# Where the key and query products of the first three pairs land in PSUM, and an early one-column Exp, in a fused attention and feed-forward kernel

## The chip, the cores and the metric

The kernel runs on one core of one Trainium2 chip. The metric is the device time of one execution in microseconds. A profiled execution gives, besides its time, a trace: every instruction of the engines TensorE (PE, with its weight loads as PEld), VectorE (DVE), ScalarE (ACT), GpSimd (POOL) and SyncE (SP) with its start, its length and what it waited for.

## What is computed

The input x has 2048 rows of 448 values in bf16. After a layer norm, two branches run side by side and are added to x. Branch A is linear attention with 16 heads of 28 and a learned feature map; branch B is a feed-forward block with SiLU.

```python
xn = _layernorm(x)
return x + _A_ref(xn, A_wqkv, A_w_phi, A_wo) + _B_ref(xn, B_w1, B_w2)
# A: q, k, v = heads of xn @ wqkv
pq = einsum("bhsd,hdf->bhsf", q, w_phi);  pk = einsum("bhsd,hdf->bhsf", k, w_phi)
phi_q = concat([softmax(pq), softmax(-pq)]);  phi_k = concat([softmax(pk), softmax(-pk)])
kv = einsum("bhsf,bhsd->bhfd", phi_k, v);  z = einsum("bhsf->bhf", phi_k)
o = einsum(phi_q, kv) / (einsum(phi_q, z) + 1e-6);  return o @ wo
# B
return silu(xn @ w1) @ w2
```

## The kernel before

**Tiles and stages.** The 2048 rows are 8 pairs of two tiles of 128 rows. Stage one loads x and w1, normalises the pairs, transposes them (xnT) and computes the first feed-forward product for pairs 0 to 5, with a SiLU on ScalarE after every unit (function ffn1_chunk). In between, w_phi is folded into the weights of queries and keys (fold), so that one product gives pk and one pq. Stage two, the one that the change touches, goes once through the pairs 0 to 7. Stage three multiplies queries with the key-value sums, divides, transposes, and adds the second feed-forward product and the product with wo, pair by pair, and stores.

**One pair of stage two.** k_macro (L877) makes three things. The keys of the pair: 14 matmuls of 448 columns in two passes of row halves (proj, contract), into two PSUM banks; then two Exps on ScalarE (exp_act, L776), one of the values and one of their negatives, out of these banks into a slot of scr or wraw (Ek). The values: 14 matmuls into banks 2 and 3, copied out by VectorE (L469). The sums of the exponentials on VectorE (L892), their reciprocals (L894), and the scaling on POOL (L900). q_group (L922) makes the queries of a group of heads c for half of all rows (pairs 0 to 3, then 4 to 7): 14 matmuls of 512 columns into two banks and two Exps into EqT. From pair 3 on, every second pair also accumulates keys with values for two earlier pairs in bank 4 (k_acc). All matmuls are issued by the helper mms (L446), all operations of ScalarE by act (L465).

**The banks.** Of the eight PSUM banks, values always have 2 and 3. Keys have 0 and 1, only those of pair 1 have 4 and 5. Queries always have 6 and 7. Bank 4 is free until the accumulation of keys with values begins in pair 3. A matmul that writes a bank anew waits until all readers of that bank's old content are through: for keys and queries that is the second of their two Exps.

**What sets the order.** The program collects operations with their data dependences; a planner orders them per engine from estimated costs. TensorE's order is tied down by a chain written out by hand: in a pair, the first pass of the keys, the first of the values, the second of the keys, the second of the values (in even pairs and in pair 1 its last step stands behind the queries' first pass), then the queries' two passes; in pairs 3, 5 and 7 the accumulation stands between the queries' two passes. On ScalarE, Exps carry order ties behind all earlier SiLUs, and later SiLUs behind the Exps, so that the function tables are switched once each way. The build puts a table load ahead of the first operation that needs another table; where that operation waits for a semaphore, the wait stands ahead of the load. The loads of w2 and wo on SyncE's queue wait for the first Exp of the keys of pairs 0 to 4.

**Names.** neghalf is a small constant tile that POOL fills at the start, and pre a two-column scratch tile: a one-column Sqrt from neghalf to pre's first column runs at the start of ScalarE's queue. silus and exps collect the SiLUs and Exps so far.

Of the kernel before, what the change touches and what calls it, by code (L numbers as in the profile page):

```python
# [8 lines left out]
ACTF = mybir.ActivationFunctionType  # L9
# [99 lines left out]
def _cols(ap):  # L109
    n = 1  # L110
    for st, cnt in list(ap.ap)[1:]:
        n *= cnt
    return n
# [219 lines left out]
def bass_parallel_sum__linear_kernel_hedgehog__dense_activation_silu__prompt_kernel(  # L333
# [21 lines left out]
    with es:  # L355
        def sb(name, shape, dt):
            return es.enter_context(nc.sbuf_tensor(name, shape, dt))
# [29 lines left out]
        pre = sb("pre", [128, 2], F32)  # L387
# [9 lines left out]
        neghalf = sb("neghalf", [128, NT], F32)  # L397
# [11 lines left out]
        psum = es.enter_context(nc.psum_tensor("psum", [128, 8 * 512], F32))  # L409
        psum16 = psum[:].bitcast(BF16)  # L410
        banks = [psum[:, i * 512:(i + 1) * 512] for i in range(8)]
# [11 lines left out]
        def d_mm(n):  # L423
            return max(n * 0.4167 + 1.0, 55.0)

        def d_act(n):
            return n / 1.2 + 170.0

        def d_dve(n, mode=1):
            return n * 1.042 / mode + 150.0  # L430

        def d_rec(n):
            return n * 6.25 + 150.0

        def d_pool(n, per=1.0):
            return n * per + 120.0
# [6 lines left out]
        def mms(parts, name, dur, mode=64):  # L443
            def fn(e):
                for dst, lhsT, rhs, start, stop in parts:
                    r = e.matmul(dst, lhsT, rhs, start=start, stop=stop, skip_group_check=True)  # L446
                return r
            return P.op("pe", dur, fn, reads=[a for p in parts for a in (p[1], p[2])],
                        writes=[p[0] for p in parts], table=mode, name=name)
# [14 lines left out]
        def act(dst, src, func, name, table=None, scale=1.0):  # L464
            return P.op("act", d_act(_cols(src)), lambda e: e.activation(dst, src, func, scale=scale),  # L465
                        reads=[src], writes=[dst], table=table, name=name)

        def copy_dve(dst, src, name, dur):
            return P.op("dve", dur, lambda e: e.tensor_copy(dst, src), reads=[src], writes=[dst], name=name)  # L469

        def xb(par, k):
            return 3 if k == 3 else (k if par == 0 else 4 + k)

        def contract(jobs, n, first, last, name, sync=None):

            passes = ([((0, 0, UP), (1, 0, LO)), ((0, 1, UP), (1, 1, LO)), ((0, 2, UP), (1, 2, LO)), ((0, 3, UP), (1, 3, LO))],
                      [((0, 0, LO), (1, 0, UP)), ((0, 1, LO), (1, 1, UP)), ((0, 2, LO), (1, 2, UP))])
            prev, done = None, []  # L480
            for q, steps in enumerate(passes):
                ops = []
                for X, W, dsts, opens, wstat in jobs:
                    for i, step in enumerate(steps):
                        parts = []
                        for par, k, r in step:
                            xx, ww = X(r, xb(par, k)), W(r, k)
                            lhsT, rhs = (ww, xx) if wstat else (xx, ww)
                            parts.append((dsts[par], lhsT, rhs, first and opens and q == 0 and i == 0,
                                          last and q == 1 and i == len(steps) - 1))  # L490
                        ops.append(mms(parts, name, d_mm(n)))
                if q == 1:
                    for o in ops:
                        o.syncs.add(prev.id)
                prev = ops[-1]
                done.append(ops)
            return done
# [220 lines left out]
        silus = []  # L718
        exps = set()
# [55 lines left out]

        def exp_act(dst, src, scale, name):  # L776
            o = act(dst, src, ACTF.Exp, name, table="exp", scale=scale)
            for s in silus:
                if s.id not in o.deps:
                    o.odeps.add(s.id)  # L780
            exps.add(o.id)
# [91 lines left out]
        def proj(p, W, b0, name):  # L873
            return contract([(lambda r, b: xnT[r, b, p, :], W,
                       [banks[b0 + par][:, 0:D] for par in range(2)], True, False)], D, True, True, name)

        def k_macro(p):  # L877
            sl = p % NEK
            kbk = 4 if p == 1 else 0
            k12 = proj(p, lambda r, k: wqk_sb[r, k, 1, :, 0:56], kbk, "pk_mm")  # L880
            kb = psum[:, kbk * 512:kbk * 512 + 1024].rearrange("p (t c) -> p t c", t=2)[:, :, 0:D]
            for s in range(2):
                exp_act(Ek[sl][:, :, s * D:(s + 1) * D], kb, 1.0 if s == 0 else -1.0, "exp_k")
            v12 = proj(p, lambda r, k: wv_sb[r, k, :], 2, "v_mm")
            vb = psum[:, 1024:2048].rearrange("p (t c) -> p t c", t=2)[:, :, 0:D].rearrange("p t (h d) -> p t h d", h=H)
            copy_dve(vaug[sl][:, :, :, 0:DH], vb, "v_ev", d_dve(896))
            for t0, t1 in ((0, 2),) if p < NPAIR - 1 else ((0, 1), (1, 2)):
                n = t1 - t0
                E4 = Ek[sl][:, t0:t1, 0:2 * D].rearrange("p t (h f) -> p t h f", f=DH)
                S3, R3 = Sk[:, sl, 32 * t0:32 * t1], Rk[:, sl, 32 * t0:32 * t1]  # L890
                S4, R4 = (a.rearrange("p (t h) -> p t h", t=n) for a in (S3, R3))
                P.op("dve", d_dve(896 * n), lambda e, S4=S4, E4=E4: e.tensor_reduce(S4, E4, AXL.X, ALU.add),  # L892
                     reads=[E4], writes=[S3], name="Sk")
                P.op("dve", d_rec(32 * n), lambda e, S3=S3, R3=R3: e.reciprocal(R3, S3), reads=[S3], writes=[R3], name="Rk")  # L894
                for s0, s1, eng in ((0, 2, "pool"),) if t0 == 0 else ((0, 1, "dve"), (1, 2, "pool")):
                    h0, h1 = 16 * s0, 16 * s1
                    E5, R5 = E4[:, :, h0:h1], R4[:, :, h0:h1]
                    R5 = R5[:, :, :, None].broadcast_to([128, n, h1 - h0, DH])
                    P.op(eng, 1100 if eng == "dve" else d_pool(448 * n * (s1 - s0), 1.72),
                         lambda e, E5=E5, R5=R5: e.tensor_tensor(E5, E5, R5, ALU.mult),  # L900
                         reads=[E5, R5], writes=[E5], name="phik")

            return k12, v12
# [16 lines left out]
            return ops  # L920

        def q_group(ch, c):  # L922
            done = contract([(lambda r, b: xnT[r, b, 4 * ch:4 * ch + 4, :].rearrange("p a c -> p (a c)"),
                       lambda r, k: wqk_sb[r, k, 0, 2 * c:2 * c + 2, :].rearrange("p j u -> p (j u)"),
                       [banks[6 + par] for par in range(2)], True, True)], 512, True, True, "pq_mm")
            src = psum[:, 6 * 512:8 * 512].rearrange("p (r c) -> p r c", r=2)
            for s in range(2):
                exp_act(EqT[:, c, s, :, ch * 512:(ch + 1) * 512], src, 1.0 if s == 0 else -1.0, "exp_q")
            return done

        for sl in range(NEK):
            P.op("pool", d_pool(32), lambda e, sl=sl: e.memset(vaug[sl][:, :, :, DH], 1.0),
                 writes=[vaug[sl][:, :, :, DH]], name="vaug1")
        P.cur_prio = 0
        chain = []
        for p in range(NPAIR):
            k12, v12 = k_macro(p)
            q12 = q_group(p // 4, p % 4)
            if p > 1 and p % 2:
                chain += [k12[0], v12[0], k12[1], v12[1], q12[0], k_acc(p - 3), k_acc(p - 2), q12[1]]  # L940
            else:
                chain += [k12[0], v12[0], k12[1], v12[1][:2], q12[0], v12[1][2:], q12[1]]
# [220 lines left out]
        for e in ("pe", "act", "dve", "pool"):  # L1163
            cnt = 0
            for oid in order[e]:
                o = ops[oid]
# [4 lines left out]
        for e in ENGINES:  # L1171
            for oid in order[e]:
                o = ops[oid]
# [88 lines left out]
```

## Time and profile before

| | us |
|---|---|
| three runs | 156.2, 156.87, 157.41 |
| median | 156.87 |
| profiled execution, its own time | 156.01 |
| span of that execution, first to last instruction | 154.3 |
| VectorE busy | 99.6 |
| ScalarE busy | 75.7 |
| GpSimd busy | 55.0 |

How to read it: the span is what the trace covers; the time of the execution has 1.7 us more around it. The granted TensorE clock of the execution was 0.998 of full speed. A row of the timeline gives start, length, engine, line, operation, output and input tiles and how many instructions were merged in it; in brackets stand the idle time of the engine ahead of it and what ended that. The length of a merged row reaches to the end of its last instruction, and two neighbours on one engine can overlap by about 0.1 us. Ends of matmuls are modelled, so distances between starts are the better measure on TensorE. In this trace a row of two Exps out of scr's or wraw's slot is the keys of a pair, and a row of two Exps into EqT its queries; the first pair's are at 45.31 and 46.92 us.

### The profile page before, as it was taken

Reading aid. Unit: us, or ns where it says so; the run is one execution under the profiler, and the core shown is the slowest. Engines: PE = TensorE matmul, PEld = TensorE weight load, DVE = VectorE, ACT = ScalarE, POOL = GpSimd, SP = SyncE. Lnnn points to the kernel's source line nnn. Section 1 sums busy time; section 2 is a strip of 40 time slices with the busy share of each in tenths; the row PEclk is TensorE's granted clock in tenths of the full one; section 3 lists DMA queues with packets and bytes.
Section 4 is the critical chain, followed back from the end, with each engine's and each line's share of the span. In section 5 each row is a group of like instructions: output and inputs, shape, how many; then the busy total and the mean of one; then the engine's idle time right before and its main releaser. Section 6 shows DMA issues by size and latency. Waiting matters only on the chain.

```text
span 154.3 us, 5662 instructions
## 1 busy us (share of the span) xinstructions
PE 149.6 (97%) x2576; PEld 98.9 (64%) x2576; DVE 99.6 (65%) x177; ACT 75.7 (49%) x89; POOL 55.0 (36%) x79
## 2 busy tenths in 40 slices
PE   6999999999998999999999999999999999999992
PEld 4698889898743445454478886645565555555672
DVE  1969788862427989494994597675665748393203
ACT  3586775569779886869869566021020202022000
POOL 7021123020100788858395024642516060605000
PEclk9999999999999999999999999999999999999999
DMA  4967754000004331210000000001101010101012
GB/s 129 339 190 185 256 170 130 4 4 4 4 0 121 123 119 59 79 44 0 4 0 4 4 0 6 4 0 64 46 18 59 0 64 0 64 2 64 0 64 60
DMA packets 8629, 9.60 MB, mean 62 GB/s; under 512 B 1501, under 2 KB 8221, under 8 KB 8605
## 3 DMA queue, kind: packets, MB, share of 16 engines
q1 hardware_dynamic: 8140, 8.96, 18.6%
q8 instruction: 20, 0.33, 0.9%
q10 hardware_dynamic: 464, 0.28, 0.6%
q14 instruction: 5, 0.03, 0.1%
HBM read 7.37 MB, written 1.84 MB: 60 GB/s over the span
## 4 chain that ended last, share of the span: by engine, by line
PE 94%; ACT 3%; issue 1%; POOL 0%; DVE 0%; ACTq 0%; POOLq 0%
PE psum L446 90%; PE psum L459 3%; ACT EqT L465 1%; ACT L465 1%; ACT scr L465 1%; ACT xnT L465 0%; DVE out_sb L1080 0%; POOL ident L501 0%; PE psum L967 0%; POOL ones_bf L500 0%; POOL neghalf L504 0%; ACTq L1202 0%; POOLq L1247 0%; POOL ones L505 0%
## 5 line engine op out<-in xcount | busy, mean ns | idle before, releaser
L446 PE MATMUL psum<-xnT,w_sb 64*128 64x256 bf16 (+1 forms) x768 | 46.8, 268 | 0.1
L446 PE MATMUL psum<-w_sb,hT 64*128 64x448 bf16 (+2 forms) x504 | 46.6, 328 | 0.0
L446 PEld LDWEIGHTS psum<-xnT,w_sb 64*128 64x128 bf16 x768 | 35.3, 94 | 5.2 <-PE psum L446 0.7
L465 ACT ACTIVATE hT<-psum 128x1024 bf16<-128x1024 f32 (+1 forms) x29 | 28.3, 995 | 13.8 <-PE psum L446 13.2
L1051 POOL TENSOR_TENSOR xn_sb<-wraw 128x448 bf16<-128x448 f32 (+4 forms) x39 | 20.7, 562 | 37.0 <-DVE wraw L1029 37.0
L446 PEld LDWEIGHTS psum<-w_sb,hT 64*128 64x128 bf16 x504 | 22.7, 94 | 16.6 <-ACT oT L465 0.4
L465 ACT ACTIVATE oT<-psum 128x896 bf16<-128x896 bf16 x8 | 7.3, 917 | 40.4 <-PE psum L459 40.4
L900 POOL TENSOR_TENSOR scr<-scr,Rk 128x1792 bf16<-128x1792 bf16 x6 | 19.3, 3211 | 18.0 <-ACT scr L465 11.3
L465 ACT ACTIVATE EqT<-psum 128x1024 bf16<-128x1024 f32 x16 | 15.5, 1023 | 5.5 <-PE psum L446 5.5
L1029 DVE TENSOR_TENSOR wraw<-psum,Gq 128x1792 f32<-128x1792 f32 (+1 forms) x9 | 16.4, 1817 | 0.9
L446 PE MATMUL psum<-xnT,wqk_sb 64*128 64x512 bf16 x112 | 14.8, 378 | 0.4 <-ACT EqT L465 0.4
L1080 DVE TENSOR_TENSOR out_sb<-psum,x_sb 128x896 bf16<-128x896 f32 (+2 forms) x9 | 8.8, 981 | 9.5 <-PE psum L446 9.4
L1016 DVE RECIPROCAL R<-psum 128x64 f32<-128x64 f32 (+1 forms) x9 | 4.6, 512 | 14.9 <-PE psum L446 14.9
L446 PE MATMUL psum<-wv_sb,xnT 64*128 64x448 bf16 x112 | 14.0, 349 | 0.0
L446 PE MATMUL psum<-wo_sb,oT 64*128 64x448 bf16 (+2 forms) x126 | 13.6, 328 | 0.0
L446 PE MATMUL psum<-wqk_sb,xnT 64*128 64x448 bf16 x112 | 13.2, 349 | 0.0
L607 DVE BATCH_NORM_STATS2 st<-x_sb 128x6 f32<-128x448 bf16 x16 | 9.8, 615 | 4.4 <-DMA x_sb<-in_A_x_dram 4.4
L892 DVE TENSOR_REDUCE Sk<-scr 128x64 f32<-128x1792 bf16 x6 | 12.1, 2013 | 0.6 <-ACT scr L465 0.6
L616 POOL TENSOR_TENSOR rstd<-ve,neghalf 128x2 f32<-128x2 f32 (+1 forms) x8 | 5.4, 670 | 19.6 <-DVE ve L615 19.6
L469 DVE CAST scr<-psum 128x896 bf16<-128x896 f32 x6 | 6.5, 1083 | 8.9 <-PE psum L446 8.9
L465 ACT ACTIVATE scr<-psum 128x896 bf16<-128x896 f32 x12 | 10.4, 922 | 0.7 <-PE psum L446 0.4
L446 PEld LDWEIGHTS psum<-xnT,wqk_sb 64*128 64x128 bf16 x112 | 4.7, 94 | 6.9 <-PE psum L446 1.7
(69 smaller groups left out, 139.6 us busy)
## 6 DMA issues: line engine op xcount, KB each, us to landing
out_dram<-out_sb SPq DMA_DIRECT2D x7, 224.0 KB, 1.9
w_sb<-in_B_w_dram SPq DMA_DIRECT2D x3, 448.0 KB, 3.3
x_sb<-in_A_x_dram SPq DMA_DIRECT2D x2, 448.0 KB, 4.3
w_sb<-in_B_w_dram SPq DMA_DIRECT2D x2, 384.0 KB, 7.2
x_sb<-in_A_x_dram SPq DMA_DIRECT2D x3, 224.0 KB, 6.1
w_sb<-in_B_w_dram SPq DMA_DIRECT2D x3, 224.0 KB, 3.3
wraw<-in_A_wqkv_dram SPq DMA_DIRECT2D x1, 672.0 KB, 4.8
w_sb<-in_B_w_dram SPq DMA_DIRECT2D x1, 576.0 KB, 4.2
```

What stands on the lines that cost most here:

```text
L446: r = e.matmul(dst, lhsT, rhs, start=start, stop=stop, skip_group_check=True)
L459: out = e.transpose(dst, src, ident[r, 64:128] if r == LO else ident[r, 0:64])
L465: return P.op("act", d_act(_cols(src)), lambda e: e.activation(dst, src, func, scale=scale), reads=[src], writes=[dst], table=table, name= ...
L469: return P.op("dve", dur, lambda e: e.tensor_copy(dst, src), reads=[src], writes=[dst], name=name)
L607: P.op("dve", 600, lambda e: e.bn_stats(st6[:, t, :], x_sb[:, t, :]), reads=[x_sb[:, t, :]], writes=[st6[:, t, :]], name="bnst")
L616: P.op("pool", 580, lambda e: e.tensor_tensor(r2, v2, nh, ALU.pow), reads=[v2, nh], writes=[r2], name="rstd")
L892: P.op("dve", d_dve(896 * n), lambda e, S4=S4, E4=E4: e.tensor_reduce(S4, E4, AXL.X, ALU.add), reads=[E4], writes=[S3], name="Sk")
L900: lambda e, E5=E5, R5=R5: e.tensor_tensor(E5, E5, R5, ALU.mult),
L1016: P.op("dve", d_rec(32 * n), lambda e, R3=R3, U=U: e.reciprocal(R3, U[:, :, :, DH + 1]), reads=[U[:, :, :, DH + 1]], writes=[r2], name="R2")
L1029: P.op("dve", d_dve(896 * n), lambda e, dsto=dsto, U=U, G3=G3, n=n: e.tensor_tensor(dsto, U[:, :, :, 0:DH], G3[:, :, :, None].broadcast_to ...
L1051: lambda e, dst=dst, a0=a0, a1=a1: e.tensor_tensor(dst, a0, a1, ALU.add),
L1080: P.op("dve", d_dve(2 * (c1 - c0)), lambda e: e.tensor_tensor(dst, ob, xs, ALU.add), reads=[ob, xs], writes=[dst], name="out_ev")
```

## The change

For pairs 1 and 2 keys and queries get other banks. Each cell gives the two banks that the products land in:

| pair | keys before | keys after | queries before | queries after |
|---|---|---|---|---|
| 0 | 0, 1 | 0, 1 | 6, 7 | 6, 7 |
| 1 | 4, 5 | 4, 5 | 6, 7 | 0, 1 |
| 2 | 0, 1 | 6, 7 | 6, 7 | 4, 5 |
| 3 to 7 | 0, 1 | 0, 1 | 6, 7 | 6, 7 |

In the second group of queries (pairs 4 to 7) the number 4 * ch + c is 4 to 7, so nothing changes there. Besides, a one-column Exp from neghalf into pre's second column is tied behind the SiLUs recorded by then, which are those of stage one, and every Exp of keys and queries is tied behind it; SiLUs of stage three stay behind all Exps. The order of the instructions on TensorE, VectorE, POOL and SyncE is the same as before; ScalarE's has the one added instruction, with the table load ahead of it.

```diff
@@ -775,6 +775,7 @@
 
         def exp_act(dst, src, scale, name):
             o = act(dst, src, ACTF.Exp, name, table="exp", scale=scale)
+            o.odeps.add(pre_exp.id)
             for s in silus:
                 if s.id not in o.deps:
                     o.odeps.add(s.id)
@@ -876,7 +877,7 @@
 
         def k_macro(p):
             sl = p % NEK
-            kbk = 4 if p == 1 else 0
+            kbk = {1: 4, 2: 6}.get(p, 0)
             k12 = proj(p, lambda r, k: wqk_sb[r, k, 1, :, 0:56], kbk, "pk_mm")
             kb = psum[:, kbk * 512:kbk * 512 + 1024].rearrange("p (t c) -> p t c", t=2)[:, :, 0:D]
             for s in range(2):
@@ -920,10 +921,11 @@
             return ops
 
         def q_group(ch, c):
+            qb = {1: 0, 2: 4}.get(4 * ch + c, 6)
             done = contract([(lambda r, b: xnT[r, b, 4 * ch:4 * ch + 4, :].rearrange("p a c -> p (a c)"),
                        lambda r, k: wqk_sb[r, k, 0, 2 * c:2 * c + 2, :].rearrange("p j u -> p (j u)"),
-                       [banks[6 + par] for par in range(2)], True, True)], 512, True, True, "pq_mm")
-            src = psum[:, 6 * 512:8 * 512].rearrange("p (r c) -> p r c", r=2)
+                       [banks[qb + par] for par in range(2)], True, True)], 512, True, True, "pq_mm")
+            src = psum[:, qb * 512:(qb + 2) * 512].rearrange("p (r c) -> p r c", r=2)
             for s in range(2):
                 exp_act(EqT[:, c, s, :, ch * 512:(ch + 1) * 512], src, 1.0 if s == 0 else -1.0, "exp_q")
             return done
@@ -932,6 +934,9 @@
             P.op("pool", d_pool(32), lambda e, sl=sl: e.memset(vaug[sl][:, :, :, DH], 1.0),
                  writes=[vaug[sl][:, :, :, DH]], name="vaug1")
         P.cur_prio = 0
+        pre_exp = act(pre[:, 1:2], neghalf[:, 0:1], ACTF.Exp, "pre", "exp")
+        pre_exp.odeps.update(o.id for o in silus)
+        exps.add(pre_exp.id)
         chain = []
         for p in range(NPAIR):
             k12, v12 = k_macro(p)
```

## The prediction

> **What bounds the kernel now.** I read the page first, for the engine that is busy and the chain that ended last.
>
> ```profile
> span 154.3 us, 5662 instructions
> PE 149.6 (97%) x2576; PEld 98.9 (64%) x2576; DVE 99.6 (65%) x177; ACT 75.7 (49%) x89; POOL 55.0 (36%) x79
> ...
> PE 94%; ACT 3%; issue 1%; POOL 0%; DVE 0%; ACTq 0%; POOLq 0%
> ```
>
> TensorE is busy in 97% of the span and carries 94% of the chain. So only time that TensorE loses, and the kernel's two ends, can be won. Where does it lose any? The waits of TensorE's matmuls over the whole span are two lines:
>
> ```profile
> PE psum L446 <- POOL ones L505: 1.4, 1, 1.4
> PE psum L446 <- ACT EqT L465: 0.4, 1, 0.4
> ```
>
> The first lies at the start, far from the change. The second is the one place where an exponential (EqT is written by the query Exps alone in this stage) holds TensorE up. The chain of waits in order of time shows that place:
>
> ```profile
> 44.02 1.28 ACT L465
> ...
> 46.92 1.96 ACT EqT L465 x2
> 48.88 0.05 issue
> 48.93 36.54 PE psum L446 x496
> ```
>
> Between the last SiLU unit and 48.93 us the chain leaves TensorE: it runs through the load of the Exp table, the two key Exps of pair 0, the two query Exps of pair 0, and only then TensorE goes on. Behind 48.93 there are 36.54 us of TensorE in one piece, so a shift there passes through. How much was lost? The timeline of TensorE from the last value step of a pair to the first query step, for pairs 0 and 1:
>
> ```profile
> 43.77 0.54 PE L446 MATMUL psum<-wv_sb,xnT 64*128 64x448 bf16 x4
> 44.15 1.03 PE L446 MATMUL psum<-xnT,wqk_sb 64*128 64x512 bf16 x8
> ...
> 47.98 0.54 PE L446 MATMUL psum<-wv_sb,xnT 64*128 64x448 bf16 x4
> 48.93 1.04 PE L446 MATMUL psum<-xnT,wqk_sb 64*128 64x512 bf16 x8 [0.40 <-ACT EqT L465]
> ```
>
> The distance is 0.38 us in pair 0 and 0.95 in pair 1: 0.57 lost (the 0.40 of the wait starts only at the modelled end of the matmul before). The busy time by stretches, cut from the first key step of one pair to that of the next, says the same:
>
> ```profile
> 41.69:45.90 4.21, 4.21 (x46) 1.96 (x42) 1.00 0.00 0
> 45.90:50.69 4.79, 4.39 (x45) 1.88 (x42) 1.00 0.33 97
> 50.69:54.90 4.21, 4.21 (x44) 1.96 (x42) 1.00 0.36 113
> ```
>
> A pair costs 4.21 us, pair 1 cost 4.79. Pair 0 starts on banks that nothing of this stage has used, so 4.21 is TensorE's own pace. The loss is 4.79 - 4.21 = 0.58 us, and it is all that waits for banks cost in this stage. The third number from the end is the granted clock: 1.00 in each.
>
> **The change, part by part: the one-column Exp.** ACT's timeline around it, then the one-column operation that the kernel has already, and another table load:
>
> ```profile
> 41.89 1.02 ACT L465 ACTIVATE hT<-psum 128x1024 bf16<-128x1024 f32 x1 [0.79 <-PE psum L446]
> 44.02 1.28 ACT L465 ACT_TABLE_LOAD   x1 [1.10 <-PE psum L446]
> 45.31 1.73 ACT L465 ACTIVATE scr<-psum 128x896 bf16<-128x896 f32 x2
> 46.92 1.95 ACT L465 ACTIVATE EqT<-psum 128x1024 bf16<-128x1024 f32 x2
> ...
> 50.89 1.94 ACT L465 ACTIVATE EqT<-psum 128x1024 bf16<-128x1024 f32 x2 [0.40 <-PE psum L446]
> ...
> 55.11 1.94 ACT L465 ACTIVATE EqT<-psum 128x1024 bf16<-128x1024 f32 x2 [0.41 <-PE psum L446]
> ```
> ```profile
> 2.54 0.20 ACT L465 ACTIVATE pre<-neghalf 128x1 f32<-128x1 f32 x1
> ...
> 6.92 0.60 ACT L465 ACTIVATE xnT<-psum 128x512 bf16<-128x512 bf16 x1 [0.26 <-PE psum L459]
> 7.53 1.28 ACT L465 ACT_TABLE_LOAD   x1
> ```
>
> Now the load stands behind the wait for the keys: the last SiLU ends at 41.89 + 1.02 = 42.91, ACT idles 1.10, and loads from 44.02 to 45.30. The listing of the built kernel's order has one added ACT instruction, the load comes before it without a wait, and there is no second load. So the load runs from 42.92 to 44.20, the Exp (0.20, from the row of the one-column Sqrt) to 44.41, and the first key Exp starts at about 44.42, when its keys have been there since 44.02. That is 45.31 - 44.42 = 0.89 us earlier. By itself this ends the stall: the query Exps of pair 0 can then start as soon as their matmuls are through, at about 46.11 (pair 1's Exps at 50.89 came 1.96 after its first query step at 48.93; pair 0's first query step was at 44.15), and end at 46.11 + 1.95 = 48.06, before the 48.36 (47.98 + 0.38) at which TensorE wants the bank.
>
> Its own 0.20 us costs nothing: it lies in the 1.10 us of idle time. Without that cover it would delay the key Exps by 0.20.
>
> **The rotation.** Queries of pair 1 go to banks 0 and 1, so they wait for the key Exps of pair 0, which end at 45.31 + 1.73 = 47.04 even in the old timing: 1.32 us before 48.36. The rotation too ends the stall alone. The other moves, each by what TensorE waited for at that place before: keys of pair 2 wait for query Exps of pair 0 (already waited for by the queries of pair 1 before); queries 2 for key Exps 1 (before: query Exps 1, later in ACT's order); keys 3 for query Exps 1 (before: key Exps 2, later); queries 3 for key Exps 2 (before: query Exps 2, later); the first accumulation of keys with values, in bank 4, for query Exps 2, which the queries of pair 3 ahead of it waited for before. So in TensorE's unchanged order no wait is for later work than it was. Two waits are new as instructions, at keys 2 and at that accumulation; the whole TensorE queue stands behind each, but both Exps end over 1 us ahead. Two rows more of the timeline:
>
> ```profile
> 54.75 0.63 PEld L446 LDWEIGHTS psum<-wqk_sb,xnT 64*128 64x128 bf16 x8 [0.18 <-ACT scr L465]
> ...
> 58.51 0.98 PE L446 MATMUL psum<-scr 128*58 128x112 bf16 x32
> ```
>
> The query Exps of pair 0 end at 48.06 for keys that are due at 50.69 - 0.58 = 50.11, and those of pair 2, all of it 0.58 earlier, at 55.11 + 1.94 - 0.58 = 56.47 for an accumulation due at 58.51 - 0.58 = 57.93. I cost them at nothing, with 0.2 us (the one-column instruction) as the upper end for both.
>
> **What is late next.** The values stay in banks 2 and 3, emptied by VectorE. Its timeline:
>
> ```profile
> 45.41 1.09 DVE L469 CAST scr<-psum 128x896 bf16<-128x896 f32 x1 [3.36 <-PE psum L446]
> 47.07 2.02 DVE L892 TENSOR_REDUCE Sk<-scr 128x64 f32<-128x1792 bf16 x1 [0.57 <-ACT scr L465]
> 49.12 0.55 DVE L894 RECIPROCAL Rk<-Sk 128x64 f32<-128x64 f32 x1
> 50.20 1.09 DVE L469 CAST scr<-psum 128x896 bf16<-128x896 f32 x1 [0.52 <-PE psum L446]
> ```
>
> The copy of pair 1's values came at 50.20, 0.52 after VectorE was free; with TensorE 0.58 earlier it is wanted at 49.62. VectorE is free for it when the reciprocal ends, 49.12 + 0.55 = 49.67, which is 4.36 us after the first key Exp starts (45.31). So with the load at its old place the copy would be late by 49.67 - 49.62 = 0.05, and the rotation alone would bring 0.53; with the Exp at 44.42 VectorE has 0.84 us to spare. Here the one-column Exp is the cover of the rotation. Two more things move with the key Exps: SyncE issues the first load of w2 behind the first of them, about 0.9 us earlier, into a tile that nobody else uses yet, and POOL's scaling follows VectorE's reciprocal. Both at nothing.
>
> **The sum.** 0.58 gained, 0 paid. Bounds: above, 0.58 plus the 0.18 us by which weight loads for keys of pair 3 waited (at 54.75) for a key Exp: 0.76. Below, 0.58 less 0.2 for the waits, 0.38. I take 0.58, since pair 0, which has no such short wait, and pair 2, which ends with it, show the same 4.21. The profiled execution took 156.01 us (span 154.3, and 1.7 around it): 156.01 - 0.58 = 155.43. It was faster than the three runs (156.2 to 157.41); from their median, 156.87 - 0.58 = 156.29.
>
> [...]
>
> **The rivals.** (A) VectorE becomes the bound: the load and the Exp take longer than the rows say, the first key Exp comes after 45.26 (49.62 - 4.36), and the copy of pair 1's values is late by as much. At a start of 45.55, halfway between this point and that of rival B, the gain is 0.58 - 0.29 = 0.29: 156.6. For it speaks that the old start, 45.31, lies already past this point; against it the rows of 1.28, 0.01 and 0.20. [...]
>
> (B) The same place, on the other side: past a start of 45.84 (50.20 - 4.36) pair 1's values are copied later than before, and the kernel is slower by as much as the start is later. That takes 2.93 us from the last SiLU against 1.48 by the rows. A second load behind another wait of 1.10 would bring it: 42.91 + 1.28 + 0.20 + 1.10 + 1.28 = 46.77, a loss of 0.93: 157.8. Against it: the built order has one load, and nothing to wait for ahead of it.
>
> (C) The change doesn't do what it says: the 0.58 is lost again further on, and nothing is gained. The chain piece of 36.54 us without another engine speaks against it; 156.9.
>
> **How the numbers follow.** Forecast 0.77, A 0.12, B 0.05, C 0.06. The effect is 0.4%, below the 1% that a measurement of this kernel can tell from no change; the three runs before lie 1.2 us apart, so chance alone moves a median by half a microsecond. Range: 155.2 (the profiled run's 155.43 with the upper bound of the gain, 0.76 in place of 0.58) to 157.0 (rival C with a tenth). Faster by over 1% (under 155.3) is the forecast with a median lower by chance: 0.12. Slower by over 1% (over 158.4) is B with a start past 47.4, or C with a high median: 0.05. Within 1%: 0.83.
>
> **What would show it.** In the profile after: the load of the Exp table at 42.9, right behind the last SiLU; a 0.20 us Exp; key Exps at 44.4; no wait of TensorE for EqT; the first query step of pair 1 0.38 after the last value step; 4.21 us for pair 1; span near 153.7. A first copy of values of pair 1 later than 49.7, and a wait of TensorE for it in pair 2, would show A or B. I would be wrong altogether if pair 1 took 4.21 us and a later pair more than it did.

## The result, and the profile after

In twelve executions each, the median is 155.67 us after the change against 156.54 us before. The ratio is 0.9943, 95% interval 0.9918 to 0.9968: a gain of 0.3 to 0.8%, and the predicted 0.58 us (0.37%, ratio 0.9963) lies inside. Ratios and intervals, here and below, come from the single executions of both kernels without the few slow ones (over 1.5% above the fastest of the same kernel), so they differ a little from the quotient of the two medians. The profiled execution took 155.98 us with a span of 154.2, against 156.01 and 154.3 before. By these spans alone hardly anything happened, so the stage has to be read by itself.

ScalarE's timeline of the kernel after, from the last SiLU of stage one to the query Exps of pair 0:

```profile
42.44 1.02 ACT L465 ACTIVATE hT<-psum 128x1024 bf16<-128x1024 f32 x1 [0.79 <-PE psum L446]
43.48 1.28 ACT L465 ACT_TABLE_LOAD   x1
44.78 0.20 ACT L465 ACTIVATE pre<-neghalf 128x1 f32<-128x1 f32 x1
44.88 1.71 ACT L465 ACTIVATE scr<-psum 128x896 bf16<-128x896 f32 x2
46.66 1.94 ACT L465 ACTIVATE EqT<-psum 128x1024 bf16<-128x1024 f32 x2
```

The table load stands right behind the SiLU (42.44 + 1.02 = 43.46) instead of 1.10 us behind it. All times in this trace are shifted, because the first key step came at 42.24 and not at 41.69; measured from that step, the first key Exp starts at 44.88 - 42.24 = 2.64 us instead of 45.31 - 41.69 = 3.62.

TensorE's waits over the whole span, its timeline where the stall was, and the three stretches from first key step to first key step:

```profile
PE psum L446 <- POOL ones L505: 1.4, 1, 1.4
PE psum L459 <- DVE EqT L645: 0.5, 1, 0.5
```
```profile
48.53 0.54 PE L446 MATMUL psum<-wv_sb,xnT 64*128 64x448 bf16 x4
48.91 1.03 PE L446 MATMUL psum<-xnT,wqk_sb 64*128 64x512 bf16 x8
```
```profile
42.24:46.45 4.21, 4.21 (x46) 1.96 (x42) 1.00 0.00 0
46.45:50.66 4.21, 4.21 (x44) 1.96 (x42) 1.00 0.37 111
50.66:54.88 4.22, 4.22 (x45) 1.96 (x43) 1.00 0.38 113
```

The wait for an Exp is gone from the list, the distance from the last value step to the first query step is 0.38 us, and pair 1 takes 4.21 us where it took 4.79. (The second wait in the list is VectorE in the layer norm at the start.) The chain of waits shows why the span hides this:

```profile
1.71 5.60 DMA x_sb<-in_A_x_dram
...
9.67 0.41 PE psum L459 x8
...
41.65 43.80 PE psum L446 x573
85.44 0.22 PE psum L972 x16
...
141.57 9.98 PE psum L446 x174
```

From 41.65 to 85.44 the chain is TensorE alone, in one piece: the detour over ScalarE that lay between 44.02 and 48.93 is no longer there. But its head is now a load of x that landed at 7.31 us, and everything behind it began later: the 0.55 us lost by the first key step hide the 0.58 us won behind it. The last piece of TensorE in the chain of the kernel before is

```profile
141.61 9.98 PE psum L446 x174
```

From the first key step to the end of that piece it is 151.59 - 41.69 = 109.90 us before and 151.55 - 42.24 = 109.31 after: 0.59 less, so the gain isn't lost again further on. Over all ten profiles of this study the first key step lies anywhere from 41.46 to 43.41 us; that spread is over three times the effect. There is one profile for each kernel, and no experiment tried what sets this time.

### The profile page after: what moved, and what is told of

Same layout as the page of the kernel before. It is cut to its first block, busy times and chain, and to the rows that moved or that the text cites. A ratio compares the mean times of both kernels' runs of the same rounds, so it can differ in the third digit from the quotient of the medians.

```text
span 154.2 us, 5664 instructions
## 1 busy us (share of the span) xinstructions
PE 149.6 (97%) x2576; PEld 99.1 (64%) x2576; DVE 99.6 (65%) x177; ACT 76.2 (49%) x90; POOL 55.0 (36%) x79
## 4 chain that ended last, share of the span: by engine, by line
PE 92%; DMA 4%; DVE 2%; SPq 1%; issue 0%
PE psum L446 89%; DMA x_sb<-in_A_x_dram 4%; PE psum L459 3%; DVE st L607 1%; SPq L538 1%; DVE out_sb L1085 0%; DVE mv L609 0%; DVE EqT L645 0%; DVE ve L615 0%; PE psum L972 0%
## 5 line engine op out<-in xcount | busy, mean ns | idle before, releaser
L446 PEld LDWEIGHTS psum<-wo_sb,oT 64*128 64x128 bf16 x126 | 5.9, 94 | 4.8 <-ACT oT L465 0.2
```

## The experiments

Each number called a loss below is the time by which a stretch from first key step to first key step exceeds TensorE's own 4.21 us.

**Each half alone.** The first kernel (exp_only) keeps the Exp and takes the rotation back; the second (rot_only) keeps the rotation and drops the Exp.

```diff
 # exp_only
-            kbk = {1: 4, 2: 6}.get(p, 0)
+            kbk = 4 if p == 1 else 0
-            qb = {1: 0, 2: 4}.get(4 * ch + c, 6)
+            qb = 6
 # rot_only
-            o.odeps.add(pre_exp.id)
-        pre_exp = act(pre[:, 1:2], neghalf[:, 0:1], ACTF.Exp, "pre", "exp")
-        pre_exp.odeps.update(o.id for o in silus)
-        exps.add(pre_exp.id)
```

> The one-column Exp stays, the banks are those of the kernel before. My theory (each half alone removes the same 0.58 us wait): the query Exps of pair 0 end 6.37 us after the first key step of pair 0, 0.30 us before the queries of pair 1 want banks 6 and 7; pair 1 takes 4.21 us, no wait of TensorE for EqT, the time is that of the changed kernel (0.994 of before). Rival (the rotation does it and the Exp only helps VectorE): pair 1 takes 4.79 us, time as before.

Measured: 155.75 us against 156.03, ratio 0.9963 (0.9934 to 0.9991). The busy time of pair 1 and ScalarE's query Exps of pair 0 beside TensorE's first query step of pair 1:

```profile
46.24:50.45 4.21, 4.21 (x44) 1.96 (x42) 1.00 0.40 111
```
```profile
46.45 1.94 ACT L465 ACTIVATE EqT<-psum 128x1024 bf16<-128x1024 f32 x2
```
```profile
48.70 1.03 PE L446 MATMUL psum<-xnT,wqk_sb 64*128 64x512 bf16 x8
```

The Exps end at 48.39, 0.31 us ahead of the step that needs their banks. The Exp alone is enough; the rival is out.

> The banks rotate, the one-column Exp is left out, so the table load stands behind the wait for the keys again. My theory: the wait of pair 1's queries is gone (4.21 us instead of 4.79 up to the first key step of pair 2), but the copy of pair 1's values comes at the end of the first reciprocal, so the next values start late by about 0.05 us: gain 0.53 us, 0.9966 of before. Rival (the early table load does it): time as before, pair 1 at 4.79.

Measured: 155.48 us against 156.03, ratio 0.996 (0.9926 to 0.9994). Pair 1 and pair 2:

```profile
47.63:51.84 4.21, 4.21 (x45) 1.96 (x42) 1.00 0.38 111
51.84:56.05 4.21, 4.21 (x44) 1.96 (x42) 1.00 0.38 113
```

The rotation alone is enough too. The expected 0.05 us did not show. VectorE's timeline tells why:

```profile
50.85 0.55 DVE L894 RECIPROCAL Rk<-Sk 128x64 f32<-128x64 f32 x1
51.34 1.09 DVE L469 CAST scr<-psum 128x896 bf16<-128x896 f32 x1
```

The sums of pair 0 and the same copy in the kernel after:

```profile
46.96 2.01 DVE L893 TENSOR_REDUCE Sk<-scr 128x64 f32<-128x1792 bf16 x1
...
50.17 1.09 DVE L469 CAST scr<-psum 128x896 bf16<-128x896 f32 x1 [0.61 <-PE psum L446]
```

Without the Exp the copy starts 0.06 us before the reciprocal's row ends (51.40), and so 3.71 us after pair 1's first key step at 47.63, where the kernel after has it 3.72 after (50.17 against 46.45). The two gains of 0.58 us are one gain: either half removes the whole wait, and both together bring no more.

**How far each half carries.** In these two kernels the one-column Exp is replaced by a longer one over x, into a part of EqT that is overwritten later, so the key Exps come later; the first (late4_rot) with the rotation, the second (late4_norot) without.

```diff
-        pre_exp = act(pre[:, 1:2], neghalf[:, 0:1], ACTF.Exp, "pre", "exp")
+        ld = EqT[:].rearrange("p c s t n -> p (c s t n)")[:, 12288:12288 + 448 * 4].rearrange("p (a b) -> p a b", a=4)
+        ls = x_sb[:, 0:4, :]
+        pre_exp = P.op("act", 170, lambda e: e.activation(ld, ls, ACTF.Exp), reads=[ls], writes=[ld], table="exp", name="pre")
```

> Rotated banks, and in place of the one-column Exp one over 1792 columns of x into a part of EqT that is overwritten later: about 1.68 us instead of 0.20, so the first key Exp starts about 4.1 us after the first key step of pair 0 (before 3.62, changed kernel 2.64). Theory (VectorE's copy of values is the next bound): no wait of pair 1's queries, but the copy of pair 1's values is late by about 0.5 us and the values of pair 2 start late by as much; the changed kernel plus 0.5 us, about 0.999 of before. Rival (only the banks of keys and queries count, the key Exps of pair 0 still end 0.8 us before the queries of pair 1 need them): the changed kernel's time, 0.994 of before.

> The same Exp over 1792 columns with the banks of the kernel before. Theory: the query Exps of pair 0 end 3.56 us after the first key Exp starts, the queries of pair 1 then wait about 1.06 us instead of 0.58; about 0.5 us slower than before, ratio 1.003, and VectorE's copy is not late on top of it. Rival (what counts is when the table is loaded, and it is loaded early here): the wait is shorter than before, ratio below 1.

The longer Exp took 1.70 us in both. Measured with the rotation: 155.92 us against 156.03, ratio 0.9993 (0.9972 to 1.0015); without it 156.66, ratio 1.0049 (1.002 to 1.0078). With the rotation, pairs 1 and 2:

```profile
46.28:50.49 4.21, 4.21 (x44) 1.96 (x42) 1.00 0.38 111
50.49:55.02 4.53, 4.38 (x44) 1.88 (x42) 1.00 0.34 105
```

Without it, pair 1:

```profile
46.17:51.45 5.28, 4.38 (x44) 1.88 (x42) 1.00 0.32 88
```

So the place is as the theory says, the wait of the queries without the rotation (loss 1.07, expected 1.06) and the values of pair 2 with it, and the rival that sees only the banks of keys and queries would have had no loss in pair 2. The other rival, that only the time of the table load counts, would have had a shorter wait than before without the rotation; it grew from 0.58 to 1.07. The size with the rotation is 0.32 and not 0.5. VectorE and the weight loads of the values of pair 2, with the rotation:

```profile
50.01 0.55 DVE L895 RECIPROCAL Rk<-Sk 128x64 f32<-128x64 f32 x1
50.48 1.03 DVE L469 CAST scr<-psum 128x896 bf16<-128x896 f32 x1
```
```profile
51.56 0.49 PEld L446 LDWEIGHTS psum<-wv_sb,xnT 64*128 64x128 bf16 x8 [0.59 <-DVE scr L469]
```

The copy starts 4.20 us after pair 1's first key step (46.28), 0.48 later than the 3.72 of the kernel after. Of these 0.48, 0.06 are won by the copy itself (1.03 in place of 1.09), and the other 0.10 were slack: the copy ends 0.16 us ahead of the values in the kernel after (51.26 against 51.42) and 0.05 ahead of them here (51.51 against 51.56).

**The order on VectorE.** late4_rot again, but with pair 1's values copied ahead of pair 0's reciprocal:

```diff
-            copy_dve(vaug[sl][:, :, :, 0:DH], vb, "v_ev", d_dve(896))
+            vc = copy_dve(vaug[sl][:, :, :, 0:DH], vb, "v_ev", d_dve(896))
+            if p == 1:
+                [o for o in P.ops if o.name == "Rk"][0].odeps.add(vc.id)
```

> As late4_rot, but VectorE copies the values of pair 1 ahead of the first reciprocal of pair 0 instead of behind it. Theory (the 0.32 us that late4_rot lost lies on VectorE's order: copy behind sums and reciprocal): the copy can start when the sums of pair 0 end, about 7.9 us after the first key step, which is when it is wanted; pair 2 takes 4.21 us again instead of 4.53, ratio to before 0.995. Rival (the values wait for something else that comes with the late Exps): pair 2 stays at 4.53.

Measured: 155.64 us against 156.54, ratio 0.9963 (0.9932 to 0.9993). VectorE, and pair 2:

```profile
47.41 2.02 DVE L895 TENSOR_REDUCE Sk<-scr 128x64 f32<-128x1792 bf16 x1 [1.07 <-ACT scr L465]
49.46 1.09 DVE L469 CAST scr<-psum 128x896 bf16<-128x896 f32 x1
```
```profile
49.95:54.17 4.22, 4.22 (x45) 1.96 (x42) 1.00 0.38 113
```

The 0.32 us are gone with nothing but VectorE's order changed. So the copy of the values, queued behind the sums and the reciprocal, was the wait behind the rotated banks.

**A longer Exp yet, and one move of the rotation alone.** The next two use 3584 columns (8 in place of 4 in the diff above), with the rotation (late8_rot) and without it (late8_norot); the last (q1_only) moves only the queries of pair 1.

> As late4_rot with an Exp over 3584 columns, about 3.2 us, so the first key Exp starts about 5.6 us after the first key step of pair 0. Theory (VectorE's copy of values is the bound behind the banks): the queries of pair 1 wait about 0.75 us for the key Exps of pair 0, and the values of pair 2 wait about 1.05 more for the copy of pair 1's values; 1.8 us over the changed kernel, ratio to before 1.008. Rival (only the banks of keys and queries count): 0.75 us over the changed kernel, 1.001.

Measured: 157.53 us against 156.38, ratio 1.0084 (1.0052 to 1.0117). The longer Exp took 3.19 us. Pairs 1 and 2 and TensorE's two waits:

```profile
47.22:52.23 5.01, 4.45 (x44) 1.79 (x40) 1.00 0.26 73
52.23:57.46 5.23, 4.40 (x44) 1.90 (x44) 1.00 0.35 111
```
```profile
PE psum L446 <- DVE scr L469: 0.8, 1, 0.8
PE psum L446 <- ACT scr L465: 0.6, 1, 0.6
```

Losses of 0.80 and 1.02 us, expected 0.75 and 1.05, each with the releaser that the theory named.

> The Exp over 3584 columns with the banks of the kernel before. Theory: the queries of pair 1 wait for the query Exps of pair 0, which end about 9.2 us after the first key step of pair 0, while the queries are due at 6.67: a wait of 2.6 us in place of 0.57, about 2.0 us slower than before, ratio 1.013; with rotated banks the same Exp cost 0.7 less. In some executions the granted clock falls to half for some us behind a wait this long, as it did in one profile of q1_only behind 2.2 us without matmuls, and costs about 1.7 us more. Rival (the clock's fall in q1_only had nothing to do with the length of the wait): no window below full clock here.

Measured: 158.91 us against 156.54, ratio 1.014 (1.0091 to 1.0189). Pair 1:

```profile
45.67:52.44 6.77, 4.38 (x44) 1.88 (x42) 1.00 0.23 69
```

A loss of 2.56 us, 0.74 more than with the rotation. In this profile the clock stayed at 1.00; in two of the six executions the mean granted clock was 0.988 and 0.989, at 160.76 and 159.21 us. The profile by itself looks as the rival said; the two executions speak for the theory, but there is no trace of them.

```diff
-            kbk = {1: 4, 2: 6}.get(p, 0)
+            kbk = 4 if p == 1 else 0
-            qb = {1: 0, 2: 4}.get(4 * ch + c, 6)
+            qb = {1: 0}.get(4 * ch + c, 6)
```

> The changed kernel, but only the queries of pair 1 move (to banks 0 and 1); keys and queries of pair 2 land where they did before. Theory (the rotation is one closed set of moves): the queries of pair 1 don't wait, but the keys of pair 2, in the same banks 0 and 1, must wait for the query Exps of pair 1, which end about 3.9 us after the first query step, while these keys are due 1.75 after it: about 2.2 us lost at the first key step of pair 2, ratio to before 1.010. Rival (the one move that meets the old wait is enough): the changed kernel's time, 0.994.

Measured: 158.15 us against 156.38, ratio 1.0124 (1.0065 to 1.0183). The profiled execution took 160.06 us, with a slower clock later on (last section); up to the first key step of pair 2 its clock was 1.00. TensorE at the first key step of pair 2, and the stretch up to it:

```profile
53.05 0.93 PE L446 MATMUL psum<-wqk_sb,xnT 64*128 64x448 bf16 x8 [2.04 <-ACT EqT L465]
```
```profile
46.63:53.05 6.42, 4.38 (x46) 1.88 (x42) 1.00 0.50 144
50.85:53.05 2.20, 0.16 (x4) 0.01 (x2) 1.00 0.74 209
53.81:58.06 4.25, 4.25 (x28) 1.76 (x26) 0.60 0.01 4
```

A loss of 2.21 us, expected 2.2. The one move that meets the old wait makes a worse one two steps on; the moves of pair 2 gain nothing by themselves, but without them the first can't be made. The third row belongs to the last section.

Now the profiles with the old banks or the whole rotation, and VectorE's own order, together. The first key Exps of the five without the one-column Exp, in the order rot_only, late4_rot, late4_norot, late8_rot, late8_norot, are

```profile
47.04 1.73 ACT L465 ACTIVATE scr<-psum 128x896 bf16<-128x896 f32 x2
46.21 1.71 ACT L465 ACTIVATE scr<-psum 128x896 bf16<-128x896 f32 x2
46.10 1.71 ACT L465 ACTIVATE scr<-psum 128x896 bf16<-128x896 f32 x2
48.65 1.71 ACT L465 ACTIVATE scr<-psum 128x896 bf16<-128x896 f32 x2
47.09 1.71 ACT L465 ACTIVATE scr<-psum 128x896 bf16<-128x896 f32 x2
```

and the first key steps of pair 0 are at 43.41, 42.07, 41.96, 43.01 and 41.46 us. By how long after the first key step of pair 0 the first key Exp starts (the losses of pairs 1 and 2 added; with the old banks pair 2 has none):

| first key Exp | kernel | loss, old banks | loss, rotated banks |
|---|---|---|---|
| 2.64 to 2.65 us | one-column Exp | 0 | 0 |
| 3.62 to 3.63 us | no early Exp | 0.58 | 0 |
| 4.14 us | 1792 columns | 1.07 | 0.32 |
| 5.63 to 5.64 us | 3584 columns | 2.56 | 1.82 |

Each column grows by 1 us per us past a point: about 3.05 us with the old banks (three kernels), 3.82 with the rotated ones (two kernels). The kernel before stood 0.58 past the first point. The Exp moves the start back by 0.98; the rotation moves the point out by 0.77; either is more than 0.58.

## Why the prediction was right, step by step

- **The loss of 0.58 us and its cause.** Right: pair 1 went from 4.79 to 4.21 us, and no later pair grew: pair 3 takes 5.17 us in both traces (54.90 to 60.07 before, 54.88 to 60.05 after), and pairs 4 to 6 agree within 0.01. So the load of w2 and POOL's scaling, which move with the key Exps, cost nothing there, as forecast. The size in the trace is 0.58; the medians differ by 0.87, whose interval (0.5 to 1.3 us) holds 0.58. The 156.29 us was built on a median of three runs; with twelve, the median before is 156.54, and 156.54 - 0.58 = 155.96 would have been closer to 155.67; the 0.29 us left over lie inside the interval. The 1% that the prediction took for the least that can be told apart was too coarse: here the interval is 0.25% to either side.
- **The one-column Exp.** Right in place, slightly off in size: the key Exps came 0.98 us earlier, not 0.89. The Exp's row is 0.20, but the key Exp started 0.10 after that row's start (44.78 to 44.88), so here it delayed the key Exps by half its row; the load took 1.28, as before, with a gap of 0.02 us on either side (43.46 to 43.48, 44.76 to 44.78), where the rows of the kernel before show 0.01 (7.52 to 7.53, 45.30 to 45.31). That either half alone ends the stall is now shown, not only argued.
- **The rotation's other moves at nothing.** Right for the changed kernel: no new wait in pairs 2 and 3. What the prediction argued by order only, the kernel with one move confirmed from the other side: left in their old banks, the keys of pair 2 wait 2.2 us.
- **VectorE is late next.** The right place, mis-sized. The prediction let the copy become late from a first key Exp at 3.57 us on (45.26 - 41.69); the runs show 3.82, because the copy starts 0.06 to 0.08 before the reciprocal's row ends, is 0.06 shorter where it is late, and has 0.10 of slack ahead of the values. So "the Exp is the cover of the rotation" was wrong for this kernel: the rotation needs no cover at a start of 3.63. It would at 4.14. The spare time with the Exp was mis-sized too, 0.61 us (the idle time ahead of the copy at 50.17) and not 0.84. In the kernel after, the sums of pair 0 start 2.08 us after the first key Exp (46.96 - 44.88) and not 1.76 as before (47.07 - 45.31), since they now follow directly on VectorE's copy of pair 0's values (45.95 + 1.09 = 47.04).
- **Rival A** (a dearer load, VectorE as the bound) did not happen, but its mechanism is real: late4_rot is this case. **Rival B**, the same place until it turns to a loss, is late8_rot; its turning point, by the line of the table, is 3.82 + 0.58 = 4.40 us after the first key step, and not 4.15. **Rival C** is out: TensorE's chain from 41.65 to 85.44 has nothing else in it, and the 0.59 us are still there at its end.
- **The span near 153.7** was wrong, 154.2: the forecast took the time up to the first key step as fixed, and it varies by nearly 2 us from profile to profile (41.46 to 43.41).

## What to carry to other kernels

Where one engine sets the pace, count a stage's loss as its period minus the period of an iteration that cannot wait, and stop there: two remedies for one wait gave one gain here, 0.58 us by either half and 0.58 by both. A remedy that moves buffers has to be followed to the next user of each buffer, and to the next engine in line, since it gives slack and not time: here 0.77 us of it, up to the next queue. And when the gain is smaller than what the start of the kernel scatters (0.58 us against 1.95 here), compare stretches between two events of the same stage, not spans.

## What the runs showed of the hardware

In one profile a long wait of TensorE was followed by a slower clock. In the kernel with one move TensorE had next to no matmuls for 2.2 us (50.85 to 53.05), and about a microsecond after it went on, the granted clock fell. The last row again in finer steps, with the clock as the third number from the end:

```profile
53.00:54.00 1.00, 0.95 (x10) 0.50 (x12) 0.92 (x2) 0.00 (x0) 0.03 (x1) 1.00 0.00 0
54.00:55.00 1.00, 1.00 (x10) 0.47 (x8) 0.00 (x0) 0.00 (x0) 0.97 (x1) 0.61 0.00 0
55.00:56.00 1.00, 1.00 (x8) 0.36 (x6) 0.00 (x0) 0.00 (x0) 1.00 (x1) 0.50 0.06 16
56.00:57.00 1.00, 1.00 (x8) 0.47 (x6) 0.00 (x0) 0.73 (x1) 1.00 (x1) 0.50 0.00 0
57.00:58.00 1.00, 1.00 (x8) 0.37 (x6) 0.00 (x0) 0.99 (x2) 0.24 (x1) 0.68 0.00 0
58.00:59.00 1.00, 1.00 (x14) 0.36 (x10) 0.54 (x1) 0.00 (x0) 0.00 (x0) 1.00 0.56 127
```

Two steps read 0.50 from end to end. If the mixed steps beside them (0.61 and 0.68) hold nothing but 0.50 and 1.00, half clock held for (0.39 + 0.50 + 0.50 + 0.32) / 0.50 = 3.4 us, from about 54.2 to 57.6: an estimate from these rows. The steps from the first values of pair 2 to the last took 4.25 us (53.81 to 58.06), where the kernel after needs 2.56 (51.42 to 53.98): 1.7 us more, on top of the 2.2. It doesn't always happen: of the six executions of this kernel two ran at a mean clock of 0.989 (160.06 and 159.61 us) and the others at 1.0 (157.50 to 158.76). After waits of 2.4 us (late8_norot's profile) and of 0.8 (late8_rot's) the trace shows no fall: the clock reads 1.00 in every step up to 58 us. A low mean clock also came in a kernel without such a wait in this stage (0.58 us in its profile): of 68 executions of the kernel before, measured beside the experiments, one ran at 0.987 (159.68 us). Among all executions with a clock on record, 4 of the 12 of q1_only and late8_norot lie at 0.988 or 0.989, and only that one of the 151 others lies below 0.998. So a wait of over 2 us seems to make a fall likelier; that it causes it is not shown, and only one of the five has a trace. What decides between the executions was not tried.
